# Moving the first two units' v copies and one normalization off VectorE, and values by the whole tile

## The chip, the cores and the metric

The kernel runs on one core of a Trainium2 chip. Five engines work side by side on it: TensorE (PE in the profile, with its weight loads under PEld), VectorE (DVE), ScalarE (ACT), GpSimd (POOL) and SyncE (SP). The metric is the device time of one execution in microseconds, lower is better: 324.95 us before, the median of three runs from 324.91 to 325.01 us.

## The reference

Sliding-window causal attention over 8 sequences of 576 positions with 8 heads of 64, and then a gated feed-forward layer on its output:

```python
rel = pos[:, None] - pos[None, :]
mask = (rel >= 0) & (rel < 64)
attn = softmax(where(mask, q @ k.T / 8, -1e9))        # per head
x = (attn @ v)                                        # heads side by side: 4608 x 512
out = (np.maximum(x @ w_gate, 0.0) * (x @ w_val)) @ w_out   # 512 -> 1536 -> 512
```

## The kernel before

**Tiling.** A *unit* is 192 positions of one sequence, all 8 heads. Two units make a tile of 384 tokens for the feed-forward part; there are four such tiles and then six of 512 tokens, whose attention is done in a wider form. The feed-forward width of 1536 is 12 blocks of 128, loaded in three groups of four per matrix (`G3`, `V3`, `O3`). The weights arrive by GpSimd's DMA queue, as 16-bit values converted from the 32-bit inputs, and stay in SBUF.

**One unit of attention** runs through these helpers, each with a half `hh` of four heads where it says so:

- `u_st`: scores on TensorE, as small matmuls of 32 rows (L233). `u_bias` has put the mask's bias into the bank beforehand for units 0 and 1.
- `u_exp`: the exponential on ScalarE, PSUM to SBUF (L267).
- `v_spread`: copies of v (L200, L202). v comes from memory in 128-row windows at every second step of 64; the windows between are put together by copying the upper half of one to the lower half of the next and the other way round. Its engine is a parameter, as is the range of heads.
- `u_pv`: probabilities times v on TensorE, four column groups at a time (L293). A column of ones beside v gives the row sums.
- `u_recip`: reciprocal of the row sums on VectorE (L310 for a half, L307 for both halves).
- `u_norm`: the product of PSUM and reciprocal, rearranged, to `x` (L317, VectorE).
- `u_turn`: VectorE's 32x32 block transpose into `xt`, the transposed tokens that the feed-forward matmuls stream (L327).

**The feed-forward part** is `hidden` and then `output`. `hidden` takes blocks of weights; for each it computes the gate matmuls (`wg`) and the value matmuls (`wv`) into PSUM banks `h` (L468), `relu` on ScalarE to `r_sb` (L453), and `gate` on VectorE, the product of `r_sb` and the value bank (L456). For tile 0 and the first four blocks it is called with two spans, `((0, U), (U, TT))`: gates of unit 0, gates of unit 1, values of unit 0, values of unit 1, two blocks sharing a bank of 2 x 192 columns. With that, unit 0 can enter the feed-forward part before unit 1's `xt` is there.

**Order.** It is written out by hand: each engine executes its instructions in the order in which the program emits them. From L533 on the opening (attention of units 0 and 1) is emitted directly. Later attention work is put into a `Weaver`, a list of actions with due times, which are emitted between feed-forward matmuls as an estimated TensorE clock passes them. `w_need` advances that clock to the time at which a weight block is assumed to have landed.

**PSUM.** The four banks of the pool `f_ps` (tag `h`) are shared in turn by the scores of unit 0, the products `pv` of units 0 and 1, and then the banks `h`. `heat` issues matmuls on zeros (L207) whose result nobody reads.

Of the kernel before, what the change touches and what calls it, by code (L numbers as in the profile page):

```python
# [10 lines left out]
FP32 = mybir.dt.float32  # L11
FP16 = mybir.dt.float16
ACT = mybir.ActivationFunctionType
MUL = mybir.AluOpType.mult
# [30 lines left out]
def kernel(  # L45
# [10 lines left out]
    nc = tc.nc  # L56
    B, H, S, D = q.shape
# [3 lines left out]
    U = 192  # L61
    UB = S // U
    NU = B * UB
    NC = DM // 128
    NF = DF // 128
    G = 4
    scale = 1.0 / float(D) ** 0.5
    TT = 2 * U
    WT = 512
# [6 lines left out]
    consts = ctx.enter_context(tc.tile_pool(name="consts", bufs=1))  # L76
# [3 lines left out]
    a_n = ctx.enter_context(tc.tile_pool(name="a_n", bufs=2))  # L80
    x_sb = ctx.enter_context(tc.tile_pool(name="x_sb", bufs=3))
    g_sb_p = ctx.enter_context(tc.tile_pool(name="g_sb", bufs=2))
# [4 lines left out]
    wg = persist.tile([128, NC, DF], FP16)  # L87
    wv = persist.tile([128, NC, DF], FP16)
# [41 lines left out]
    W = Weaver()  # L130
    units = {}
# [3 lines left out]
    def xt_tile(t):  # L135
        if t not in xts:
            xts[t] = x_sb.tile([128, NC, WT], FP16, name="xt")
        return xts[t]
# [14 lines left out]
    def w_need(wt, f):  # L153
        while (wt.name, f) not in w_done:
            W.pop()
        W.advance(w_done[wt.name, f])
# [37 lines left out]
    def v_spread(u, copy=None, h0=0, h1=H):  # L194

        b, uu = divmod(u, UB)
        t = v16s[b % 2]
        copy = copy or nc.vector.tensor_copy
        for g0, g1 in (((0, 3),), ((4, 5),), ((6, 7),))[uu]:
            copy(t[64:128, g0:g1:2, h0:h1, 0:64], t[0:64, g0 + 1:g1 + 1:2, h0:h1, 0:64])  # L200
        for g0, g1 in (((2, 3),), ((4, 5),), ((6, 9),))[uu]:
            copy(t[0:64, g0:g1:2, h0:h1, 0:64], t[64:128, g0 - 1:g1 - 1:2, h0:h1, 0:64])  # L202

    def heat(n, to, start=True):

        for _ in range(n):
            nc.tensor.matmul(to, zero[:, 0:128], zero[:, 0:to.shape[1]], start=start, stop=start, skip_group_check=not start)  # L207
# [6 lines left out]
    def one_bank(name):  # L214
        return f_ps.tile([128, 512], FP32, name=name, tag="h")

    def two_banks(name):
        return a_ps.tile([128, 2, 512], FP32, name=name, tag="a")
# [40 lines left out]
    def p_of(u, h, w):  # L259
        return units[u]["p"][h % G][:, UB * (h // G) + w]  # L260
# [13 lines left out]
    SB = U // 32  # L274

    def u_pv(u, hhs=(0, 1), banks=None):

        d = units[u]
        if "pv" not in d:
            if banks:  # L280
                d["pv"] = [one_bank("pv") for _ in range(2)]
            else:
                both = two_banks("pv")
                d["pv"] = [both[:, hh] for hh in range(2)]
                d["both"] = both
        for hh in hhs:
            to = d["pv"][hh]
            for w in range(UB):
                b, vw = divmod(UB * u + w, NG)
                for s in range(2):  # L290
                    for j in range(G):
                        c = VW * (2 * w + s)
                        nc.tensor.matmul(  # L293
                            to[32 * j:32 * j + 32, c:c + D + 1], p_of(u, G * hh + j, w)[:, 32 * s:32 * s + 32],
                            v16s[b % 2][:, vw, G * hh + j, 0:D + 1],
                            start=True, stop=True, skip_group_check=True)
        return 0.27 * len(hhs)

    def pv_of(d, u, hh):
        return d["pv"][hh][:, 0:SB * VW].rearrange("p (s c) -> p s c", c=VW)  # L300

    def u_recip(u, hhs=(0, 1)):
        d = units[u]
        if "r" not in d:
            d["r"] = a_n.tile([128, 2, SB, 1], FP32, name="r")
        if len(hhs) == 2:
            nc.vector.reciprocal(d["r"], d["both"][:, :, 0:SB * VW].rearrange("p a (s c) -> p a s c", c=VW)[:, :, :, D:D + 1])  # L307
        else:
            hh = hhs[0]
            nc.vector.reciprocal(d["r"][:, hh], pv_of(d, u, hh)[:, :, D:D + 1])  # L310

    def u_norm(u, hh):

        d = units[u]
        if "x" not in d:
            d["x"] = a_n.tile([128, 2, SB, 2, D // 2], FP16, name="x")
        nc.vector.tensor_tensor(d["x"][:, hh], pv_of(d, u, hh)[:, :, 0:D].rearrange("p s (c e) -> p s e c", e=2),  # L317
                                d["r"][:, hh, :, :, None].to_broadcast([128, SB, 2, D // 2]), MUL)

    def u_turn(u, hhs=(0, 1)):  # L320

        d = units[u]
        c0 = U * (u % 2)
        h0, h1 = hhs[0], hhs[-1] + 1
        for hh in range(h0, h1):
            dst = xt_tile(u // 2)[:, 2 * hh:2 * hh + 2, c0:c0 + U].rearrange("p e (s c) -> p s e c", c=32)
            nc.vector.transpose(dst, d["x"][:, hh])  # L327
        if h1 == 2:
            del units[u]
            normed[0] = (u + 1) // 2 - 1  # L330
# [101 lines left out]
    gs = {}  # L432
# [5 lines left out]
    def hidden(t, spans, f0=0, f1=NF, each=1):  # L438

        if t not in gs:  # L440
            gs[t] = g_sb_p.tile([128, NF, WT], FP16, name="g_sb"), {}
        g_sb, done = gs[t]
        xt = xt_tile(t)
        n = spans[0][1] - spans[0][0]

        w = 512 // n
        each = max(each, w)

        def part(tile):
            return tile[:, 0:w * n].rearrange("p (w n) -> p w n", w=w)  # L450

        def relu(r_sb, h1):
            nc.scalar.activation(part(r_sb), part(h1), ACT.Relu)  # L453

        def gate(f, c0, r_sb, h2):
            nc.vector.tensor_tensor(g_sb[:, f:f + w, c0:c0 + n], part(r_sb), part(h2), MUL)  # L456
            done.update(dict.fromkeys(range(f, f + w), c0 + n))

        for fb in range(f0, f1, each):
            r_sbs = {}  # L460
            for i, wt in enumerate((wg, wv)):
                for c0, f in ((c0, f) for c0, _ in spans for f in range(fb, fb + each, w)):
                    h = f_ps.tile([128, 512], FP32, name=f"h{i}", tag="h")
                    for b in range(w):
                        W.advance(W.clock)
                        w_need(wt, f + b)
                        for c in range(NC):
                            nc.tensor.matmul(h[:, b * n:b * n + n], wt[:, c, (f + b) * 128:(f + b) * 128 + 128],  # L468
                                             xt[:, c, c0:c0 + n], start=(c == 0), stop=(c == NC - 1))
                        W.clock += 4 * (n + 7) / 2400.0  # L470
                    if i == 0:
                        r_sb = r_sbs[c0, f] = f_sb.tile([128, WT], FP32, name="r_sb", bufs=6)
                        W.at(W.clock, lambda r_sb=r_sb, h=h: relu(r_sb, h))
                    else:
                        W.at(W.clock, lambda f=f, c0=c0, r_sb=r_sbs[c0, f], h=h: gate(f, c0, r_sb, h))

    def out_mm(t, op, sub, f):
        g_sb, done = gs[t]
        while done.get(f, 0) < sub * 128 + 128:
            W.pop()  # L480
        w_need(wo, f)
        nc.tensor.matmul(op, g_sb[:, f, bass.ds(sub * 128, 128)], wo[:, f],  # L482
                         start=(f == 0), stop=(f == NF - 1))
        W.clock += 519 / 2400.0
# [11 lines left out]
    def output(t, subs=None):  # L496
        for sub in range(widths[t] // 128) if subs is None else subs:
            op = op_tile()
            for f in range(NF):
                if f % 4 == 0:  # L500
                    W.advance(W.clock)
                out_mm(t, op, sub, f)
            out_evac(t, op, sub)
# [29 lines left out]
    with tc.manual_schedule():  # L533
        G3, V3, O3 = ([(wt, src, f0, f0 + 4) for f0 in (0, 4, 8)]
                      for wt, src in ((wg, moe_w_gate), (wv, moe_w_val), (wo, moe_w_out)))
        act, dve, pool = nc.scalar.copy, nc.vector.tensor_copy, nc.gpsimd.tensor_copy
# [32 lines left out]
                for i in range(G):  # L569
                    u_exp(u, i, (hh,))  # L570
        for hh in range(2):
            v_spread(0, dve, G * hh, G * hh + G)
            u_pv(0, (hh,), True)
        v_spread(1, pool)
        for hh in range(2):
            u_recip(0, (hh,))
            u_norm(0, hh)
        u_turn(0)
        for hh in range(2):
            u_pv(1, (hh,), True)  # L580
        heat(1, units[1]["st"][3])
        for hh in range(2):
            u_recip(1, (hh,))
            u_norm(1, hh)
        u_turn(1)
        w_load(*G3[1], 20.3)
        w_load(*V3[1], 22.8)
        v_load(2)
# [69 lines left out]
        W.at(15.0, lambda: loads(3, 70.0))  # L658
        T = 67.0
        W.advance(15.3)  # L660
        hidden(0, ((0, U), (U, TT)), 0, 4, 4)
        hidden(0, ((0, TT),), 4, NF, 4)
        hidden(1, ((0, U),), each=4)
        output_by_rows(0)
# [39 lines left out]
```

The softmax here doesn't subtract the row's maximum and nothing guards it: scores larger than these inputs give would overflow.

## Time and profile before

| what | before |
|---|---|
| time, median of three runs | 324.95 us |
| profiled span | 323.3 us |
| PE busy | 313.7 us (97%) |
| PEld busy | 168.4 us (52%) |
| DVE busy | 192.1 us (59%) |
| ACT busy | 127.0 us (39%) |
| POOL busy | 93.7 us (29%) |
| PE busy in 10 to 15 us, granted clock | 3.73 of 5 us, 0.50 |
| PE busy in 15 to 20 us, granted clock | 4.90 of 5 us, 0.86 |
| PE busy in 20 to 25 us, granted clock | 5.00 of 5 us, 1.00 |

The busy shares are means over the whole span. All that the change touches is emitted for the first 21 us, so the rows for single stretches are the ones to read beside it: how long TensorE works in each, and at which share of its full clock. A wait of another engine matters where TensorE's next instruction depends on it.

### The profile page before, as it was taken

The numbers are of one execution on the slowest core, as the hardware profiler recorded it, in microseconds if no ns is written. First come the engines' busy times: TensorE is split into PE (matmuls) and PEld (weight loads), VectorE is DVE, ScalarE is ACT, GpSimd is POOL, SyncE is SP. The second block draws the span as 40 slices with busy tenths as digits, with TensorE's granted clock in tenths as the row PEclk, the third lists the DMA queues.
The fourth block names the chain that finished last, engine by engine and source line by source line (L and its number), as shares of the span: only waits on it lengthen the run. The fifth ranks groups of instructions, "written<-read, shape, count | busy, mean of one in ns | idle before, by whom it ended". The sixth has DMA issues, their size and how long they took to land.

```text
span 323.3 us, 8901 instructions
## 1 busy us (share of the span) xinstructions
PE 313.7 (97%) x3851; PEld 168.4 (52%) x3851; DVE 192.1 (59%) x370; ACT 127.0 (39%) x249; POOL 93.7 (29%) x138
## 2 busy tenths in 40 slices
PE   5699999999999999999999999999999999999995
PEld 2586958656556644454445444454445444544443
DVE  5947962687938749564755656674767146723410
ACT  3444324534424523532454234613372237223321
POOL 8766335285900390029000910071000000000000
PEclk9599999999999999999999999999999999999999
DMA  7999998989590269019900892091001200020002
GB/s 215 186 196 210 194 107 174 155 150 163 83 211 4 15 108 181 3 12 124 214 5 2 111 203 24 2 122 70 0 2 38 97 0 2 21 111 3 0 34 98
DMA packets 52488, 29.48 MB, mean 91 GB/s; under 512 B 38880, under 2 KB 43872, under 8 KB 52448
## 3 DMA queue, kind: packets, MB, share of 16 engines
q0 software_dynamic: 46688, 18.29, 48.4%
q1 hardware_dynamic: 5616, 10.55, 8.9%
q8 instruction: 30, 0.49, 0.6%
q10 hardware_dynamic: 144, 0.07, 0.1%
q14 instruction: 10, 0.08, 0.1%
HBM read 37.75 MB, written 9.44 MB: 146 GB/s over the span
## 4 chain that ended last, share of the span: by engine, by line
PE 94%; DMA 2%; POOL 2%; issue 0%; ACT 0%; DVE 0%; DVEq 0%; POOLq 0%
PE h L468 59%; PE op L482 28%; PE st L233 3%; PE pv L371 2%; DMA v<-in_v_dram 2%; PE pv L293 1%; POOL v L191 1%; DMA out_dram<-o_sb 1%; POOL k L167 0%; POOL v L200 0%; POOL v L202 0%; ACT o_sb L489 0%; POOL q L167 0%; PE st L207 0%; POOL ident L107 0%
## 5 line engine op out<-in xcount | busy, mean ns | idle before, releaser
L456 DVE TENSOR_TENSOR g_sb<-r_sb,h 128x512 f16<-128x512 f32 (+1 forms) x120 | 75.4, 631 | 86.3 <-PE h L468 84.5
L468 PE MATMUL h<-xt,wg 128*128 128x512 f16 (+2 forms) x544 | 112.5, 338 | 0.1
L468 PE MATMUL h<-xt,wv 128*128 128x512 f16 (+2 forms) x544 | 111.3, 335 | 0.0
L453 ACT ACTIVATE r_sb<-h 128x512 f32<-128x512 f32 (+1 forms) x120 | 66.7, 558 | 89.5 <-PE h L468 80.4
L482 PE MATMUL op<-wo,g_sb 128*128 128x512 f16 x420 | 93.9, 379 | 0.0
L468 PEld LDWEIGHTS <-wg 128*128 128x128 f16 x544 | 51.5, 99 | 42.8 <-issue 0.5
L468 PEld LDWEIGHTS <-wv 128*128 128x128 f16 x544 | 50.5, 98 | 40.8
L482 PEld LDWEIGHTS <-g_sb 128*128 128x128 f16 x420 | 40.3, 98 | 47.1
L191 POOL DMA_DIRECT2D v<-in_v_dram x41 | 34.5, 861 | 95.0 <-PE pv L371 90.1
L489 ACT COPY o_sb<-op 128x512 f32<-128x512 f32 x35 | 20.5, 586 | 84.7 <-PE op L482 84.5
L356 DVE TENSOR_TENSOR pw<-pw,mask 128x512 f16<-128x512 f16 x48 | 19.3, 422 | 14.6 <-ACT pw L352 14.3
L352 ACT ACTIVATE pw<-st 128x512 f16<-128x512 f32 x48 | 25.7, 605 | 5.0 <-PE st L233 4.5
L200 POOL COPY v<-v 64x512 f16<-64x512 f16 (+1 forms) x21 | 15.5, 736 | 24.3 <-DMA v<-in_v_dram 23.4
L185 DVE STREAM_TRANSPOSE kT<-k 128x576 f32<-128x576 f32 x16 | 19.9, 1245 | 0.2 <-ACT k L178 0.2
L185 DVE STREAM_TRANSPOSE qT<-q 128x576 f32<-128x576 f32 x16 | 19.3, 1237 | 0.1
L267 ACT ACTIVATE p<-st 128x384 f16<-128x384 f32 (+1 forms) x40 | 14.0, 441 | 8.2 <-PE st L233 8.2
L391 DVE TENSOR_TENSOR xw<-pv,rw 128x448 f16<-128x448 f32 (+1 forms) x36 | 16.2, 507 | 0.4
L233 PE MATMUL st<-qT,kT 32*128 32x64 f16 x1152 | 12.9, 192 | 3.5 <-DVE qT L185 3.5
L202 POOL COPY v<-v 64x512 f16<-64x512 f16 (+1 forms) x21 | 15.9, 759 | 1.0
L233 PEld LDWEIGHTS <-kT 32*128 32x128 f16 x1152 | 10.8, 94 | 10.5 <-issue 8.5
L396 DVE STREAM_TRANSPOSE xt<-xw 128x1024 f16<-128x1024 f16 x12 | 14.9, 1244 | 0.4
L272 DVE TENSOR_TENSOR p<-p,mask 128x384 f16<-128x384 f16 x24 | 9.5, 414 | 3.6 <-ACT p L267 3.5
(46 smaller groups left out, 97.9 us busy)
## 6 DMA issues: line engine op xcount, KB each, us to landing
out_dram<-o_sb SPq DMA_DIRECT2D x35, 256.0 KB, 2.8
k<-in_k_dram POOLq DMA_DIRECT2D x15, 288.0 KB, 5.7
q<-in_q_dram POOLq DMA_DIRECT2D x15, 288.0 KB, 8.6
v<-in_v_dram POOLq DMA_DIRECT2D x31, 128.0 KB, 8.9
wg<-in_moe_w_gate_dram POOLq DMA_DIRECT2D x6, 256.0 KB, 6.4
wv<-in_moe_w_val_dram POOLq DMA_DIRECT2D x6, 256.0 KB, 7.7
wo<-in_moe_w_out_dram POOLq DMA_DIRECT2D x3, 512.0 KB, 12.2
v<-in_v_dram POOLq DMA_DIRECT2D x10, 64.0 KB, 5.8
```

The source lines that it names most:

```text
L185: nc.vector.transpose(dst.rearrange("p (i j) -> p j i", i=32)[:, j0:j1], src[:, j0:j1])
L191: nc.gpsimd.dma_start(v16s[b % 2][lo:hi, g, :, 0:64], v[b, :, 64 * g - 64 + lo:64 * g - 64 + hi].rearrange("h p d -> p h d"))
L202: copy(t[0:64, g0:g1:2, h0:h1, 0:64], t[64:128, g0 - 1:g1 - 1:2, h0:h1, 0:64])
L233: return [lambda dh=dh: nc.tensor.matmul(to, kTs[b % 2][rows, hh, 64 * w:64 * w + 128, dh], qTs[b % 2][rows, hh, 64 * w:64 * w + 64, dh], ...
L352: nc.scalar.activation(d["p"][g].rearrange("p n c -> p (n c)"), d["st"][g], ACT.Exp, scale=scale)
L356: nc.vector.tensor_tensor(p, p, mask[:, None, :].to_broadcast([128, 2 * QW, 64]), MUL)
L391: nc.vector.tensor_tensor(d["x"][:, hh, s0:s1], pv[:, :, 0:D].rearrange("p s (c e) -> p s e c", e=2), d["r"][:, hh, s0:s1, :, None].to_bro ...
L453: nc.scalar.activation(part(r_sb), part(h1), ACT.Relu)
L456: nc.vector.tensor_tensor(g_sb[:, f:f + w, c0:c0 + n], part(r_sb), part(h2), MUL)
L468: nc.tensor.matmul(h[:, b * n:b * n + n], wt[:, c, (f + b) * 128:(f + b) * 128 + 128], xt[:, c, c0:c0 + n], start=(c == 0), stop=(c == NC ...
L482: nc.tensor.matmul(op, g_sb[:, f, bass.ds(sub * 128, 128)], wo[:, f], start=(f == 0), stop=(f == NF - 1))
L489: nc.scalar.copy(o_sb, op)
```

## The change

It takes work off VectorE in the opening, whose instructions for unit 0 and unit 1 stand one behind the other ahead of unit 1's `xt`. Four things are edited.

- The v copies of unit 0 for the second four heads go from VectorE to GpSimd. Those of unit 1, which GpSimd did for all heads at once, are split: the first four heads on GpSimd, the second four on ScalarE.
- The normalization of unit 1's second half goes to ScalarE: `u_norm_act`, six activations of 64 columns that copy from PSUM with a scale read from the reciprocals. Unit 1's reciprocals are both emitted with the second half's first.
- In emission order unit 1's `u_pv` now stands ahead of unit 0's reciprocals. TensorE's own order stays the same: both units' products, one `heat`, then the gates.
- `hidden_first` replaces `hidden` for the first four blocks of tile 0. Gates are computed by units as before. Values are computed for the whole tile, 384 columns in one matmul and one block to a bank. The relu results are kept in two tiles laid out so that the product for a block reads both units at once.

```diff
+    def u_norm_act(u, hh):
+        d = units[u]
...
+        for s in range(SB):
+            nc.scalar.activation(d["x"][:, hh, s], pv[:, s, 0:D].rearrange("p (c e) -> p e c", e=2), ACT.Copy,
+                                 scale=d["r"][:, hh, s])
...
+    def hidden_first(t, f1):
...
+        for c0 in (0, U):
+            for f in range(0, f1, 2):
+                h = one_bank("h")
+                for b in range(2):
...
+                        nc.tensor.matmul(h[:, b * U:b * U + U], wg[:, c, (f + b) * 128:(f + b) * 128 + 128],
+                                         xt[:, c, c0:c0 + U], start=(c == 0), stop=(c == NC - 1))
...
+        for f in range(f1):
+            h = one_bank("h")
...
+                nc.tensor.matmul(h[:, 0:TT], wv[:, c, f * 128:f * 128 + 128], xt[:, c, 0:TT], start=(c == 0), stop=(c == NC - 1))
...
         for hh in range(2):
-            v_spread(0, dve, G * hh, G * hh + G)
+            v_spread(0, (dve, pool)[hh], G * hh, G * hh + G)
             u_pv(0, (hh,), True)
-        v_spread(1, pool)
+        for hh in range(2):
+            v_spread(1, (pool, act)[hh], G * hh, G * hh + G)
+            u_pv(1, (hh,), True)
+        heat(1, units[1]["st"][3])
         for hh in range(2):
             u_recip(0, (hh,))
             u_norm(0, hh)
-        u_turn(0)
         for hh in range(2):
-            u_pv(1, (hh,), True)
-        heat(1, units[1]["st"][3])
+            u_turn(0, (hh,))
+        u_recip(1, (1,))
+        u_norm_act(1, 1)
+        u_recip(1, (0,))
+        u_norm(1, 0)
         for hh in range(2):
-            u_recip(1, (hh,))
-            u_norm(1, hh)
-        u_turn(1)
+            u_turn(1, (hh,))
...
-        hidden(0, ((0, U), (U, TT)), 0, 4, 4)
+        hidden_first(0, 4)
```

## The prediction

> **What bounds the kernel now.** I read the page's chain of waits first, then the same chain for the first 34 us.
>
> ```profile
> PE 94%; DMA 2%; POOL 2%; issue 0%; ACT 0%; DVE 0%; DVEq 0%; POOLq 0%
> ```
>
> ```profile
> 11.99 0.64 POOL v L200
> ...
> 12.69 0.62 POOL v L202
> ...
> 13.35 0.74 PE pv L293 x39
> 14.09 0.54 PE st L207
> ...
> 14.67 2.25 PE h L468 x15
> ...
> 17.03 9.48 PE h L468 x81
> ```
>
> (Start, length, what.) TensorE's stream sets the end: from 14.67 us on it is gap-free but for one hole near 17 us, so a microsecond won or lost ahead of 21 us reaches the end, unless a transfer takes it back. Before it, unit 1's products wait for GpSimd's copies (13.31 us).
>
> Second, the timeline from 11 us (start, length, engine, line; TensorE's two rows end the list).
>
> ```profile
> 11.61 1.89 ACT L267 ACTIVATE p<-st 128x192 f16<-128x192 f32 x8 [0.40 <-PE st L233]
> ...
> 13.48 0.56 DVE L317 TENSOR_TENSOR x<-pv,r 128x384 f16<-128x384 f32 x1
> 13.96 1.03 DVE L327 STREAM_TRANSPOSE xt<-x 128x384 f16<-128x384 f16 x2
> ...
> 14.91 0.16 DVE L310 RECIPROCAL r<-pv 128x6 f32<-128x6 f32 x1
> 15.10 0.56 DVE L317 TENSOR_TENSOR x<-pv,r 128x384 f16<-128x384 f32 x1
> 15.57 0.18 DVE L310 RECIPROCAL r<-pv 128x6 f32<-128x6 f32 x1
> 15.79 0.56 DVE L317 TENSOR_TENSOR x<-pv,r 128x384 f16<-128x384 f32 x1
> ...
> 16.27 1.03 DVE L327 STREAM_TRANSPOSE xt<-x 128x384 f16<-128x384 f16 x2
> ...
> 18.50 2.80 PE L468 MATMUL h<-xt,wv 128*128 128x192 f16 x32
> ...
> 21.14 2.76 PE L468 MATMUL h<-xt,wg 128*128 128x384 f16 x16
> ```
>
> VectorE is busy without a break until 17.30 us, when unit 1's `xt` is complete. From these rows come TensorE's prices at full clock: 32 matmuls of 192 columns from 18.50 to 21.14 are 82.5 ns each; 16 of 384 from 21.14 to 23.74 (next wv row) are 162.5 ns. At half clock the opening's `heat` weight loads stand 0.427 us apart for 512 columns, so 192 cost 160 ns.
>
> Third, the granted clock in narrow stretches (TensorE busy, instructions, clock, DMA share, GB/s).
>
> ```profile
> 9.50:9.75 0.25, 0.00 (x0) 0.69 2.35 149
> ...
> 16.40:16.45 0.05, 0.05 (x3) 0.79 1.50 246
> 16.45:16.50 0.05, 0.05 (x3) 1.00 1.16 184
> ```
>
> It falls to half at 9.60 and returns at 16.42, 6.82 us later. Prices check the hole: from 14.67 to 16.42 run 10.9 cold gates, the other 5.1 of unit 0 end at 16.84; unit 1 starts at 17.03 (0.19 lost), and its 48 matmuls take 3.96 to 20.99, yet end at 21.14 (0.15 lost, the second transpose at 17.30). **The hole is 0.34 us.**
>
> Fourth, weights. GpSimd's waits show when the third gate group lands:
>
> ```profile
> 26.86 0.92 POOL L191 DMA_DIRECT2D v<-in_v_dram  x1 [0.52 <-DMA wg<-in_moe_w_gate_dram]
> 26.92 2.77 PE L468 MATMUL h<-xt,wg 128*128 128x384 f16 x16
> ```
>
> The second half of it is there by 26.83; the third matmul, at 26.92 + 0.33, is the first to need it. A stream earlier by over 0.4 us would wait here.
>
> [...]
>
> [...] In the trace the copy begun under VectorE work took 0.642 us against 0.61 elsewhere: nothing much.
>
> **The change part by part.**
>
> *v copies of unit 0, second half.* Two rows leave VectorE: 0.29 + 0.22 us at 11.62 to 12.16. They bring nothing: VectorE then waits for TensorE's products until 12.56 (0.40 idle). GpSimd needs 0.61 + 0.40 (512 and 256 columns; 256 by the slope from 0.61 to 1.04 for 512 and 1024). It is idle from 10.15, the loads land 5.6 to 6.4 us after issues at 4.0 and 4.9, so near 10.7: done by 11.8, before the products that need them (12.65, after their exponentials). Hidden. Contention could shift it half a microsecond and still hide it.
>
> *v copies of unit 1.* GpSimd's half is 0.40 + 0.40 after the landing, 11.99 to 12.8 (before 13.31), so the first half's products follow at once, 13.08 to 13.42 (48 took 0.68 from 13.35, so 0.34 a half). ScalarE's half queues behind the exponentials that end at 13.50: two copies of 256 columns, each 0.40, overlapped, end at 14.11. **This is a new wait:** the second half's products run from 14.15 to 14.49, not to 14.03; behind them on TensorE stand `heat` (0.43) and all gates. Unit 0's `xt` (14.45, 14.99) is then no wait, and gates start at 14.95, 0.28 us later than 14.67. Up to 16.42 this costs half, since they are cold.
>
> *Normalization.* VectorE keeps two reciprocals (to 15.31), one product (15.35 to 15.91) and two transposes; the first is over at 16.4. ScalarE's six activations of 64 columns start at 15.13. [...] I take 16.48. The last transpose then runs from 16.52 to 17.07. The relus behind it on ScalarE start at 16.5 instead of 16.20, and no bank is wanted from them before 18.3: hidden.
>
> *Values by the tile.* 16 x 162.5 ns for 32 x 82.5: 2.60 for 2.64, 0.04 saved. VectorE's products for a block now come after both units' relus, which are over by then. Hidden.
>
> *Reordering of emission and an earlier issue of later loads.* GpSimd issues the second gate group 0.45 us earlier; the DMA share is above 1 throughout, so I count no gain.
>
> *Sum.* Gates from 14.95: 9.2 cold, 6.8 warm end at 16.98. Unit 1 needs its second transpose at 17.15: there since 17.07, no hole. Then 16 x 82.5 ns and 2.60: 20.90 for 21.14, **0.24 us won.** [...] I forecast 0.2 won: 324.75. That is within 0.2% (0.65 us).
>
> **Rivals.**
>
> [...]
>
> [...]
>
> *The relief is whole.* ScalarE's copies cost nothing and gates stay at 14.67: 16.84 + 1.32 + 2.60 is 20.76, 0.38 won: 324.57. Winning over 0.65 would need the third gate group earlier as well.
>
> **How the numbers follow.** Clock as before, hole closed in whole or part (324.57 to 324.9): 0.64, taking the forecast and the whole relief together (0.56 and 0.08). A window later: 0.29. Dear activations: 0.04. Something that moves the clock's edges or the transfers to give over 0.65: 0.03. So faster 0.03, same 0.64, slower 0.33. The range runs from 324.5 to 326.5: the upper case can't be left out, and its 326.36 is uncertain by the start of the gates.
>
> **What would show it.** Right: ScalarE's copies after 13.4 and products of unit 1's second half near 14.15; gates near 14.95; clock at 16.42; no hole near 17; first gate of the second group near 20.9. Wrong: half clock to 19.8; ScalarE's activations beyond 16.7; a wait of TensorE for weights.

## The result and the profile after

The changed kernel takes **326.01 us**, the median of six runs from 325.64 to 326.59; the kernel before takes 324.98 in its six runs beside them. The ratio is 1.0036, with a 95% interval of 1.0023 to 1.0049: slower. In twenty later runs of the same changed kernel (below) it was 1.0014, from 1.0005 to 1.0023. The direction holds; the size depends on where the edges of TensorE's clock fall in each run (of its 26 executions the 8 at a mean clock of 0.984 or less have a median of 326.39, the others of 325.62), which is what the experiments are about. The forecast was 324.75, a small gain.

The profiled execution took 326.42 us. The chain of waits, by engine, still belongs to TensorE:

```profile
PE 94%; DMA 2%; DVE 2%; ACT 1%; issue 0%; DVEq 0%
```

The chain in the first 34 us, in order of time (start, length, what), shows which work now leads up to the gates:

```profile
13.53 0.40 ACT v L200
...
13.96 0.41 ACT v L202
...
14.41 0.41 PE pv L293 x13
14.82 0.54 PE st L207
15.36 4.80 PE h L507 x32
20.16 2.60 PE h L516 x16
22.76 5.20 PE h L478 x32
```

Where GpSimd's copies stood before (11.99 and 12.69), ScalarE's two stand now. The 32 gates take 4.80 us; at the 82.5 ns that one took at full clock in the trace before they would take 2.64. The timeline gives the waits in front of them:

```profile
11.35 0.68 POOL L200 COPY v<-v 64x512 f16<-64x512 f16 x1 [0.91 <-DMA v<-in_v_dram]
...
13.00 0.40 POOL L202 COPY v<-v 64x256 f16<-64x256 f16 x1
...
13.45 0.52 PE L293 MATMUL pv<-v,p 128*32 128x65 f16 x24 [0.16 <-POOL v L202]
...
14.41 0.41 PE L293 MATMUL pv<-v,p 128*32 128x65 f16 x16 [0.44 <-ACT v L202]
...
15.11 1.34 ACT L327 ACTIVATE x<-pv,r 128x64 f16<-128x64 f32 x6 [0.75 <-DVE r L310]
15.16 5.00 PE L507 MATMUL h<-xt,wg 128*128 128x192 f16 x32
...
15.78 1.29 DVE L337 STREAM_TRANSPOSE xt<-x 128x384 f16<-128x384 f16 x2
...
22.60 1.63 PE L478 MATMUL h<-xt,wg 128*128 128x384 f16 x9
```

TensorE waits 0.16 us for GpSimd and 0.44 for ScalarE, and the gates start at 15.16 instead of 14.67. VectorE has unit 1's last transpose done at 17.07, as forecast, but nobody is waiting for it. The second group of gates starts at 22.60; it was 21.14. These 1.46 us are still there at the end: TensorE's last group of output matmuls starts at 318.56 for 317.10. The whole loss is made before the second group of gates.

The granted clock (stretch, TensorE busy, instructions, clock, DMA share, GB/s) says how:

```profile
9.25:9.50 0.25, 0.22 (x28) 0.90 2.42 154
...
16.25:16.50 0.25, 0.25 (x4) 0.50 1.25 205
...
19.50:19.75 0.25, 0.25 (x4) 0.62 1.24 205
```

It falls at 9.45 (0.90 over a quarter of a microsecond) and returns at 19.69, 10.24 us later; in the trace before it returned after 6.82. In a later trace of this kernel it is 6.83. These are three and two times 3.41 us, and a stretch of 3.41 us is called a window here. At 16.28, where two windows end, the clock stays at half.

### The profile page after: what moved, and what is told of

The parts are those of the page before. It is cut to its first block, busy times and chain, and to the rows that moved or that the text cites. A ratio compares the mean times of both kernels' runs of the same rounds, so it can differ in the third digit from the quotient of the medians.

```text
span 324.7 us, 8871 instructions
## 1 busy us (share of the span) xinstructions
PE 314.7 (97%) x3835; PEld 168.6 (52%) x3835; DVE 192.0 (59%) x367; ACT 129.2 (40%) x257; POOL 94.5 (29%) x140
## 4 chain that ended last, share of the span: by engine, by line
PE 94%; DMA 2%; DVE 2%; ACT 1%; issue 0%; DVEq 0%
PE h L478 57%; PE op L525 28%; PE st L233 3%; PE pv L381 2%; PE h L507 1%; DMA k<-in_k_dram 1%; PE pv L293 1%; PE h L516 1%; DVE qT L185 1%; DVE kT L185 1%; DMA out_dram<-o_sb 1%; ACT p L267 1%; DVE q L178 0%; ACT k L178 0%; ACT o_sb L532 0%
## 5 line engine op out<-in xcount | busy, mean ns | idle before, releaser
L466 DVE TENSOR_TENSOR g_sb<-r_sb,h 128x512 f16<-128x512 f32 (+1 forms) x116 | 73.1, 633 | 83.9 <-PE h L478 82.4
L478 PE MATMUL h<-xt,wg 128*128 128x512 f16 (+2 forms) x512 | 108.6, 341 | 0.0
L478 PE MATMUL h<-xt,wv 128*128 128x512 f16 (+2 forms) x512 | 108.5, 341 | 0.0
L463 ACT ACTIVATE r_sb<-h 128x512 f32<-128x512 f32 (+1 forms) x116 | 64.7, 560 | 85.7 <-PE h L478 79.0
L478 PEld LDWEIGHTS <-wg 128*128 128x128 f16 x512 | 48.2, 98 | 42.0
L478 PEld LDWEIGHTS <-wv 128*128 128x128 f16 x512 | 47.8, 98 | 40.8
L366 DVE TENSOR_TENSOR pw<-pw,mask 128x512 f16<-128x512 f16 x48 | 19.3, 422 | 14.7 <-ACT pw L362 14.3
L200 POOL COPY v<-v 64x512 f16<-64x512 f16 (+2 forms) x22 | 16.1, 730 | 23.3 <-DMA v<-in_v_dram 22.4
L202 POOL COPY v<-v 64x512 f16<-64x512 f16 (+2 forms) x22 | 16.1, 731 | 1.1
L406 DVE STREAM_TRANSPOSE xt<-xw 128x1024 f16<-128x1024 f16 x12 | 14.9, 1245 | 0.4
```

Of the source, the lines that this page charges most:

```text
L366: nc.vector.tensor_tensor(p, p, mask[:, None, :].to_broadcast([128, 2 * QW, 64]), MUL)
```

## The experiments

All are compared with runs of the kernel before on the same chip. Where an experiment is called the kernel before with one thing changed, it keeps the changed kernel's order of emission (unit 1's products ahead of unit 0's reciprocals); the versions below that equal the kernel before show that this order costs nothing that these runs can tell. The mean granted clock of an execution tells how many windows it spent at half clock. In the trace before, 6.82 us at half go with 0.989; in the changed kernel's, 10.24 us and the last 1.2 us of the span go with 0.982. Each 3.41 us in a span of 323 lower the mean by 0.0053, so 0.995 is read as one window, 0.989 as two, 0.984 or less as three or more, an estimate from these traces. Of 118 executions of the kernel before that were run beside the experiments, 3 were at 0.984 or less; their median is 325.03 us. Four others took 327.14 to 327.79 us at a clock of 0.988 to 0.990; what slowed them is not known. Of 26 executions of the changed kernel 8 were; these have a median of 326.39, the other 18 of 325.62.

### Parts of the change alone

**v copies put back.** The changed kernel with the copies of the kernel before.

```diff
-            v_spread(0, (dve, pool)[hh], G * hh, G * hh + G)
+            v_spread(0, dve, G * hh, G * hh + G)
...
-        for hh in range(2):
-            v_spread(1, (pool, act)[hh], G * hh, G * hh + G)
+        v_spread(1, pool)
+        for hh in range(2):
             u_pv(1, (hh,), True)
```

> The changed kernel with its v copies put back (all of unit 0 on VectorE, all of unit 1 on GpSimd); normalization on ScalarE and values by the tile stay. Theory A, the hole that ScalarE's copies tear into TensorE's stream moves the clock's return by a window: with the hole gone, half clock lasts two windows again (about 6.8 us), gates start near 14.7, the hole near 17 is closed, and the time is 0.1 to 0.35 us below the kernel before. Theory B, ScalarE's six activations or the values by the tile are what costs: the time stays 0.6 us or more above the kernel before.

Measured: 325.11 us, ratio 1.0001 (0.9992 to 1.0011), three windows in 1 run of 13. The loss goes with the copies. The forecast gain does not come, though: its lowest four times, 324.88 to 324.92, are not below those of the kernel before on that chip, 324.59 to 324.93.

**The copies alone,** on the kernel before:

```diff
-            v_spread(0, dve, G * hh, G * hh + G)
+            v_spread(0, (dve, pool)[hh], G * hh, G * hh + G)
...
-        v_spread(1, pool)
+        for hh in range(2):
+            v_spread(1, (pool, act)[hh], G * hh, G * hh + G)
```

> The kernel before with the v copies alone moved as in the change; normalization on VectorE, values by units. Theory A: 0.7 to 1.4 us slower than the kernel before, as the whole change or a little more, since the hole at unit 1 is not closed either; some or all runs with a third half-clock window (mean clock 0.984 for 0.989). Theory B: within 0.3 us of the kernel before.

Measured: 326.26 us, ratio 1.0035 (1.0022 to 1.0048), three windows in 4 runs of 5. The copies alone cost what the whole change costs.

**ScalarE's part of the copies alone:** the same edit with unit 0 left on VectorE.

> The kernel before with only unit 1's second half of v copied on ScalarE; unit 0 stays on VectorE, unit 1's first half on GpSimd. Theory A: ScalarE's copies, queued behind the exponentials, make the hole: 0.6 to 1.3 us slower, a third window in half or more of the runs. If GpSimd's copies for unit 0 were what mattered, within 0.2 us of the kernel before.

Measured: 325.91 us, ratio 1.0030 (1.0018 to 1.0043), three windows in 3 runs of 6. Its timeline shows the same wait as the changed kernel's, so ScalarE's copies of unit 1 suffice:

```profile
14.28 0.41 PE L293 MATMUL pv<-v,p 128*32 128x65 f16 x16 [0.56 <-ACT v L202]
```

**Values by the tile alone,** and **the normalization alone:**

```diff
-        hidden(0, ((0, U), (U, TT)), 0, 4, 4)
+        hidden_first(0, 4)
```

> The kernel before with values by the tile alone. Theory A and my price for this part: 0.04 us faster, not to be told from no change. Theory B (values by the tile hold up the banks or VectorE's products): 0.3 us or more slower.

```diff
-        for hh in range(2):
-            u_recip(1, (hh,))
-            u_norm(1, hh)
+        u_recip(1, (1,))
+        u_norm_act(1, 1)
+        u_recip(1, (0,))
+        u_norm(1, 0)
```

> The kernel before with the normalization of unit 1's second half alone on ScalarE. Both theories: unit 1's last transpose ends near 17.05 for 17.30, which shows in time only in runs whose clock returns early; 0 to 0.25 us faster. If ScalarE's six activations were a cost of the change, this would be slower than the kernel before.

Measured: 325.02 us, ratio 0.9999 (0.9985 to 1.0012), and 324.99 us, ratio 0.9994 (0.9979 to 1.0009). No run of either had three windows (0 of 13, 0 of 14). Neither part costs anything, and neither brings anything that these runs can tell.

### Is it the idle time, by way of the clock?

**The hole made without the copies.** The kernel before without its one matmul on zeros behind unit 1's products:

```diff
-        heat(1, units[1]["st"][3])
```

> The kernel before without the one matmul on zeros between unit 1's products and the gates, so that TensorE waits there for unit 0's transposes (some 0.4 us more idle), and nothing of the work that counts comes later. Theory A: it now misses a window as the changed kernel does, in a fifth to a half of the runs (mean clock 0.984), and its median rises by 0.1 to 1.0 us. Theory B: no change, or a shade faster.

Measured: 325.95 us, ratio 1.0023 (1.0012 to 1.0034), three windows in 13 runs of 22. These 13 have a median of 326.07, the other 9 of 325.43. Its profiled execution, one with two windows, shows the wait and that the gates start where they did before:

```profile
14.68 2.18 PE L478 MATMUL h<-xt,wg 128*128 128x192 f16 x16 [0.60 <-DVE xt L337]
```

A wait of 0.60 us, no useful work later, and a time like the changed kernel's. So idle time here does move the clock: three windows or more in 13 of 22 runs, for 3 of 118 with the matmul on zeros in place.

**The hole filled.** Two matmuls on zeros between the halves of unit 1's products of the changed kernel:

```diff
+            if hh == 1:
+                heat(2, units[1]["st"][0][:, 0:2 * U])
             u_pv(1, (hh,), True)
```

> The changed kernel with two matmuls on zeros of 384 columns put on TensorE between the two halves of unit 1's products, in the hole in which it waits for ScalarE's copies. They do no useful work. Theory A: the stretch is busy again, the clock returns at the same edge as before in all or nearly all runs, and the time falls by 0.6 to 1.2 us from the changed kernel, to within 0.3 us of the kernel before, though gates start as late as in the changed kernel. Theory B, only the late start of the gates costs: no change from 326.0, or slower by the matmuls added.

Measured: 325.50 us, ratio 1.0012 (1.0003 to 1.0021), three windows in 1 run of 13. The third window goes, as theory A has it, but the time comes only half the way back. In the trace the second group of gates starts at 21.18; in the next run, which adds no instruction, at 21.02. These 0.16 us are two gates (82.5 ns each) that the four added instructions push behind a stop of TensorE's stream, shown in the next part. What makes up the rest of the 0.35 us between the two medians is not shown.

**The matmul on zeros moved into the hole,** with no instruction added:

```diff
+            if hh == 1:
+                heat(1, units[1]["st"][0])
             u_pv(1, (hh,), True)
-        heat(1, units[1]["st"][3])
```

> The changed kernel with its one matmul on zeros moved from behind unit 1's products into the hole between their halves: as many instructions as the changed kernel, the copies on ScalarE unchanged. Theory A (the idle time and the late gates in half clock are the whole loss): gates start near 14.75 for 15.05 to 15.15, the idle time shrinks from some 0.9 to 0.5 us, the third window becomes rare (a tenth of the runs or fewer), and the median falls by 0.4 to 0.9 us from the changed kernel to within 0.3 us of the kernel before. Theory B (a constant cost of the copies): it stays 0.6 us or more above the kernel before.

Measured: 325.15 us, ratio 1.0001 (0.9993 to 1.0009), three windows in 1 run of 13. ScalarE's copies are all there, and the loss is gone. Its timeline:

```profile
13.66 0.61 PE L207 MATMUL st<-zero 128*128 128x512 f16 x1
14.20 0.54 PE L293 MATMUL pv<-v,p 128*32 128x65 f16 x24
14.66 1.52 PE L507 MATMUL h<-xt,wg 128*128 128x192 f16 x15
17.02 1.56 PE L507 MATMUL h<-xt,wg 128*128 128x192 f16 x17 [0.84 <-issue]
...
21.02 2.76 PE L478 MATMUL h<-xt,wg 128*128 128x384 f16 x16
```

The matmul on zeros fills TensorE's wait, and the gates start at 14.66 again. Since both change at once, this run alone does not tell the idle time from the late start; the kernel before without its matmul on zeros does.

**The changed kernel again,** unedited:

> The changed kernel itself, for more runs of it. Theory A: in about half of the runs a third half-clock window (mean clock 0.984 or less), at 326.1 to 326.6; the others at 325.5 to 325.9, since only windows that end after 17.2 hold little enough of the hole to pass, and the late gates then run cold. Theory B (a constant cost of the copies or activations): times don't follow the clock.

Measured: 325.65 us, ratio 1.0014 (1.0005 to 1.0023). Three windows came in 5 runs of 20, not in half; the times follow the clock as expected (326.16 to 326.76 with three, 324.66 to 325.87 otherwise). The profiled execution has two windows:

```profile
15.03 4.33 PE L507 MATMUL h<-xt,wg 128*128 128x192 f16 x32
...
21.79 2.44 PE L478 MATMUL h<-xt,wg 128*128 128x384 f16 x14
```

```profile
11.25:11.50 0.25, 0.25 (x44) 0.67 1.21 185
18.00:18.25 0.25, 0.25 (x4) 0.67 1.20 197
```

The clock falls at 11.33 and returns at 18.16 (timeline first, then the clock's stretches). The edges lie elsewhere than in the first traces, and the gates run cold, at half clock, until 18.16: the second group starts 0.65 us later than before, without a third window.

### Why was there no gain?

**Holding the clock up** was tried to take the windows out of the comparison: 10 and 8 short matmuls on zeros in TensorE's idle stretches around the first scores, in the kernel with the copies put back and in the changed one.

```diff
         u_bias(1)
+        heat(10, units[1]["st"][3][:, U:2 * U], False)
...
     for hh in range(2):
+            if hh == 1:
+                heat(8, units[0]["st"][0][:, U:2 * U], False)
         for u in range(2):
```

> The changed kernel with its v copies put back, and with 10 and 8 matmuls on zeros of 192 columns in TensorE's idle stretches before and after the first scores (they add zero to banks that hold the bias), so that no window goes idle. If the windows decide: full clock from some 5 to 8 us on without a break in most runs (mean clock 0.99 to 1.0), gates of unit 0 done by 16.2, then a wait for unit 1's last transpose near 17.05; the first gates of the second group start near 20.85. 0.1 to 0.3 us faster than the kernel before and little spread between runs, unless the third group of gate weights, which lands near 26.9, takes a part back.

> The whole changed kernel with the same matmuls on zeros as the run before it; ScalarE's copies and the hole behind them stay. Theory A (the hole costs by way of the clock alone): with the clock held up, the hole and the late gates (near 14.8 at full clock, unit 0 done by 16.2) are hidden behind unit 1's last transpose near 17.07, and the time is that of the run before it within 0.15 us, some 1.0 us below the changed kernel. Theory B (the copies cost by the late start itself): 0.4 us or more above the run before it.

Measured: 329.22 us, ratio 1.0122 (1.0100 to 1.0143), and 329.41 us, ratio 1.0122 (1.0099 to 1.0145). Both expectations missed. In both traces TensorE stood still ahead of the last of unit 1's products, until 17.11, with the idle time put down to "issue", that is, to nothing that the profile shows. That pointed to the instruction stream. In the kernel of values by the tile the stop comes behind 15 gates, and in that with two more matmuls on zeros (four instructions) behind 13. First that of the values, then the filled one:

```profile
14.68 2.06 PE L507 MATMUL h<-xt,wg 128*128 128x192 f16 x15
17.03 1.64 PE L507 MATMUL h<-xt,wg 128*128 128x192 f16 x17 [0.30 <-issue]
```

```profile
14.96 1.24 PE L507 MATMUL h<-xt,wg 128*128 128x192 f16 x13
17.01 1.73 PE L507 MATMUL h<-xt,wg 128*128 128x192 f16 x19 [0.82 <-issue]
```

The same place in TensorE's stream, some 446 instructions in, and the same time.

**More instructions, same work.** The kernel before with its opening matmuls on zeros cut into shorter ones:

```diff
-        heat(6, units[0]["st"][3])
+        heat(24, units[0]["st"][3][:, 0:128])
```

> The kernel before with the six matmuls on zeros of 512 columns at the start cut into 24 of 128 columns: the same columns in the same time, 36 instructions more. Theory I: TensorE's stop comes 36 instructions earlier in the work, inside the last product of unit 1 near 14, and lasts to 17.0; gates start near 17.6 and the kernel is 3.5 to 4.5 us slower. Theory II: no change, within 0.2 us.

Measured: 329.51 us, ratio 1.0131 (1.0116 to 1.0145). The work is the same; only the number of instructions grew:

```profile
12.01 2.05 PE L293 MATMUL pv<-v,p 128*32 128x65 f16 x95
17.11 0.24 PE L293 MATMUL pv<-v,p 128*32 128x65 f16 x1 [3.05 <-issue]
...
17.68 5.33 PE L478 MATMUL h<-xt,wg 128*128 128x192 f16 x32
22.80 1.37 PE L478 MATMUL h<-xt,wv 128*128 128x192 f16 x12
```

The gates start 3.0 us later, and all 32 run cold, 0.160 us each from 17.68 to 22.80. Worked out from the 12 values that start between 22.80 and 24, the clock returns near 23.2.

**Fewer instructions.** The kernel with the copies put back, two opening matmuls less (four instructions):

```diff
-        heat(6, units[0]["st"][3])
+        heat(4, units[0]["st"][3])
```

> The changed kernel with its v copies put back, and four matmuls on zeros at the very start of TensorE's stream in place of six: four instructions fewer ahead of the gates. Theory I (the hole near 17 us is TensorE's instruction stream: in every trace so far it stops at the same place of the stream, some 446 instructions in, and goes on at 17.0): the stop moves from behind 15 gates to behind 17, where unit 1's tokens (17.05) are the limit, so in a run with an early clock the second group starts near 20.85, and the lowest times fall by 0.1 to 0.3 us. Theory II (the hole is unit 1's tokens alone): no change from the kernel with six.

Measured: 325.12 us, ratio 1.0002 (0.9993 to 1.0010). Half of it came true:

```profile
14.69 2.04 PE L507 MATMUL h<-xt,wg 128*128 128x192 f16 x17
17.28 1.40 PE L507 MATMUL h<-xt,wg 128*128 128x192 f16 x15 [0.56 <-issue]
```

The stop moved from behind 15 gates to behind 17, as theory I said, but it ended at 17.28 instead of 17.0, after unit 1's tokens (17.06 in this trace), and took the gain along. One of the 13 runs had a mean clock of 1.000, no window at half clock at all, and at 326.55 us was the slowest; it has no trace, so why is open.

**What ends the stop?** It lasts 3.05 us in the kernel with more instructions. The traces have a queue of instructions, which doesn't name the engine; in the trace before it moved 30 packets with 0.49 MB, 16 KB each. It moves one such block near the stop. Here is its row in this last trace in 14.90 to 14.95 us (packets, MB, share of the 16 engines; one packet's whole time is counted where it starts):

```profile
q8 instruction: 1, 0.02, 121.8%
```

In nine traces with a visible stop, that of the kernel before among them, the block starts between 14.35 and 14.95, and TensorE goes on 2.2 to 2.45 us after its start: 14.7 and 17.03 with the values by the tile, 14.9 and 17.28 here. The next run asked whether the weight transfers ahead of it hold it up; to the kernel with more instructions it adds, ahead of the second group of weights:

```diff
+        nc.gpsimd.tensor_copy(late, xt_tile(0)[:, 3, 160:162])
         w_load(*G3[1], 20.3)
```

> The kernel with 36 instructions more (24 short matmuls on zeros), and GpSimd's issue of the second group of weights held until unit 0's tokens are there (near 15.0 for 13.3). If TensorE's stop waits for an instruction transfer behind the weight transfers issued before it, TensorE goes on earlier than 17.1, by 0.3 us or more. If the time of going on is set otherwise, it stays within 0.1 us of 17.1. The kernel as a whole may be slower than the one it is made from by the later weights.

Measured: 328.63 us (two runs), ratio 1.0105 (1.0086 to 1.0123).

```profile
16.60 0.24 PE L293 MATMUL pv<-v,p 128*32 128x65 f16 x1 [2.76 <-issue]
```

TensorE goes on 0.51 us earlier, and the block starts at 14.37, 0.3 earlier. But in this trace GpSimd's first copies, which wait for v, began 0.2 us earlier too, before the edit can act. That the later loads freed the way is possible and not shown; that the stop ends 2.2 to 2.45 us after the block starts is what all nine traces agree on. That this block holds the instructions that TensorE waits for is inferred from this and from the count of instructions, not shown.

## Why the prediction was wrong

The time lay inside the range, and a clock that comes a window later, to which the prediction gave 0.29, is what came in 8 of 26 runs, the profiled one among them; the forecast itself, a gain of 0.2 us, was wrong in sign. By its steps:

- **"Clock as before": the step that failed.** I took the edges of one trace (9.60 and 16.42) for the kernel's own. The edges are an execution's: in two executions of the changed kernel the clock fell at 9.45 and 11.33 and returned at 19.69 and 18.16. What the change altered is the share of executions that spend a third window at half clock: 3 of 118 before, 8 of 26 after. The 18 others are slower than before as well (325.62 for 325.03), so the median's loss is not the third window alone. In the two traces of such runs, this kernel's and that of ScalarE's part of the copies, the clock returned late, at 18.16 and, worked out from the 32 gates between 15.03 and 19.24 (0.160 us each cold, 0.0825 at full clock), near 18.3. The right forecast was a mixture, with a median between its parts.
- **Which busy share brings the clock back stays open.** No run shows a share that decides it, so the 326.36 at the top of the range was my estimate. By the prediction's own prices (24 products in 0.34 us) TensorE waited from 13.08 to 13.45 and from 13.79 to 14.41 in the profiled execution, 0.99 us for the 0.73 forecast (13.42 to 14.15). In the trace before, TensorE was busy for 3.30 of the 3.41 us from 13.01 to 16.42, where the clock returned, and for 1.85 from 9.60 to 13.01, where it stayed at half. No share alone divides the traces. By the profile's count TensorE was busy for 2.81 of 3.41 us from 12.87 to 16.28 in the changed kernel, after which the clock stayed at half, and for as long in the last cold window of the kernel without its matmul on zeros, after which it returned, at 16.12. The changed kernel first, then the other:

```profile
12.87:16.28 3.41, 2.81 (x78) 0.50 1.24 205
```

```profile
12.71:16.12 3.41, 2.81 (x78) 0.50 1.23 203
```

- **The size of a late clock was right, in part by luck:** 326.36 is 1.41 us above the time before, and 1.46 were found in the profiled execution. The gates started 0.21 us later than forecast, and the clock returned at 19.69, ahead of the 19.8 in the prediction's last line, which nearly cancel. The median is smaller because only some executions lose the window.
- **"Gates from 14.95": mis-sized.** They started at 15.16. ScalarE's copies, which the last products wait for, took 0.40 us each as forecast, but began at 13.53 and stood 0.43 us apart; the overlap that ends them at 14.11 was my estimate, and no run shows it: they ended at 14.36. v for unit 0 also landed later than my 10.7 (GpSimd began at 11.35), so GpSimd's last copy ended at 13.40, not 12.8. That made the wait of 0.16 us, but did not set the start of the gates.
- **"The hole is 0.34 us" and closes with unit 1's tokens: the second step that failed.** The hole belonged to TensorE's instruction stream. It stood in the chain that I showed: the row at 14.67 counts 15 gates, while unit 0 has 16, and the sixteenth needs nothing from unit 1. So 49 matmuls, not 48, follow from 17.03; at 82.5 ns they end at 21.07, and only 0.07 us up to 21.14 is left for unit 1's tokens to take. Tokens that are ready at 17.07 for 17.30 can win no more than that, and the normalization alone wins nothing that its runs can tell.
- **Right in size:** ScalarE's six activations (no run made by then shows the 16.48 of the forecast, an estimate; they took 1.34 us and ended at 16.45), the last transpose (17.07), values by the tile (21.11 for 21.14, 0.03 saved; forecast 0.04), and GpSimd's copies for unit 0, hidden behind the exponentials.
- **A slip without effect:** VectorE is not busy without a break until 17.30; the 0.40 us of waiting before 12.56, which the prediction itself names, lies in between.
- **The late gates.** I priced a late start at half its length because the gates are cold up to 16.42. In the trace whose clock returns at 18.16 the gates start 0.36 us late (15.03 for 14.67) and the second group 0.65 us late. At the prediction's prices half the late start is 0.19 us; the rest is the clock's later return. The kernel with the normalization alone, which has no new wait ahead of its gates, spreads without a third window too: 324.87 to 325.57 us in 14 runs, the slowest at a mean clock of 0.989.

No version tried beats the kernel before by more than these runs can tell. Putting the matmul on zeros into the hole makes the changed kernel its equal.

## What to carry to other kernels

Where TensorE still runs at half clock, as here until 16.42 us in the trace before, price a new wait twice: as time, and by what it may do to the clock's return, which came at 19.69 in one execution of the changed kernel and at 18.16 in another; take a distribution from many runs, not edges from one trace. Here a matmul on zeros was worth more inside the wait than behind it (325.15 for 325.65 us). Before a stall is put down to the operand that arrives last, count the instructions up to it: here the stall stayed at the same place in the stream and ended at nearly the same time (16.60 to 17.28) in different kernels, which pointed to the supply of instructions, and more matmuls on zeros ahead of it made it worse (329.51 for 325.09).

## What the runs showed of the hardware

- With one matmul on zeros left out, which made TensorE wait 0.60 us in the trace kept, 13 of 22 runs, by their mean clock, spent three windows (3.41 us each) or more at half clock; with it, 3 of 118 did. The busy share of a window did not decide alone: after 2.81 of 3.41 us the clock returned in one trace and stayed at half in another.
- TensorE's stream stopped some 446 instructions in until 16.6 to 17.3 us in nine traces, 2.2 to 2.45 us after a 16 KB instruction block had begun to move. Thirty-six short instructions more, doing the same work, cost 4.4 us (329.51 for 325.09), since the stop then came in front of all gates and all 32 gates ran at half clock, from 17.68 to 22.80.
